# A 0/1 table multiplied onto the state decays, in place of a bias product on TensorE, in a linear-attention and Fourier-mixing kernel

## The chip, the core and the metric

The kernel runs on one core of a Trainium2 chip. The metric is device microseconds of one execution, the lower the better. A profile is one execution recorded by the hardware. Engines are named as in it: PE is TensorE (PEld its weight loads), ACT is ScalarE, DVE is VectorE, POOL is GpSimd, SP issues most DMAs.

## What is computed

Four batches, eight heads, 768 positions, 48 channels in a head (384 in all), float32 in and out. A linear attention with a decay for every channel of the key runs over the positions; its output then goes through a Fourier mixing and a two-layer network:

```python
for t in range(S):
    cur = np.einsum('bhd,bhe->bhde', u[None] * kt, vt)
    y[:, :, t] = np.einsum('bhd,bhde->bhe', rt, state + cur)
    state = wt[:, :, :, None] * state + np.einsum('bhd,bhe->bhde', kt, vt)

X = np.fft.fft(x, axis=1)
X = np.fft.fft(X, axis=2)
u = x + np.real(X)
un = (u - mean(u)) / np.sqrt(var(u) + 1e-06)
out = u + np.maximum(un @ w_ch1, 0.0) @ w_ch2
```

## The kernel before

**Chunks.** A batch is cut into six chunks of 128 positions. In a chunk the decays are summed as logarithms: a product with a triangular mask on PE gives the running sum at each position, and its exponentials scale r and k, so that the recurrence becomes three products: scores (k by r, L1120), masked by DVE (L1130); scores by v (L1185); and the state carried in from the chunk ahead, by r (L1182). The chunk's keys by its values (L1157) are added to the state in a PSUM bank, and DVE multiplies the whole with the chunk's total decay (L1165). The last chunk of a batch hands on no state.

**Total decays.** Two heads share a block of 128 partitions: the lower 64 belong to one, the upper 64 to the other. Function `total` in `attention` makes a row of eight numbers for each partition, one for each head: four products (L1006) sum the logarithms over the 128 positions, two columns at a time, and a partition gets a sum also in the column of the head it does not belong to. Ahead of them one product of the unit matrix `IDB` with a table `PB` of 0 and -200 (L1003, eight columns) writes -200 into those places, so that the exponential makes them zero. The row stands in columns 384 to 391 of the bank that holds a running sum, and ACT takes its exponential into the tail of tile `E2` (`we`), alone (L1024) or with the 384 in front of it (L1019). There are three ways for a chunk's sums, `sum_two`, `sum_add` and `sum_key`; the first uses one more product of 384 columns (L1015), the second an addition on DVE (L1029).

**Batch 0** goes in pairs of chunks (function `paired`, lines 857 to 965), with loads of two chunks each (L648) and its own bias product (L870), which is not touched. The tables of sines and the masks are made at the same time, on DVE, POOL and ACT. PE's first products (L1464, and NW products L1507 on constants) compute nothing that is used.

**After a batch's attention** follow: folding into even and odd parts (L600, `sd` and `xf`), products with cosine and sine tables (L1261, L1266), eviction and reversal (`hcs`, `hcr`, L1289 to L1293), the second transform (L1305, L1314), the sum with x, the moments (L1362, L1364), normalizing, transposing, and the two layers (L1412, then relu on ACT at L1420 or DVE at L1418, then L1431), whose result is scaled and added (L1440) and stored (L1451).

**The order.** All operations are recorded first; each engine then runs a list of them written out in the table `ORDER`, and the semaphores follow from the data. The batches overlap: while PE works at the layers of one batch, DVE, ACT and POOL do the attention of the next. For many operations the lists also choose the engine (helpers `vec`, `evict`: DVE or POOL, ACT or DVE) and the way (`choose`). An operation on POOL waits for the last DVE operation ahead of it in the plan that is marked with `port`; those are the ones that take their operands from SBUF alone. Helper lines therefore stand for many operations: L600 is every addition or product of two tensors made by `tt`, L604 and L605 are `tensor_scalar`, L611 is a fill, L614 and L623 are on ACT.

Of the kernel before, what the change touches and what calls it, by code (L numbers as in the profile page):

```python
# [7 lines left out]
ALU = mybir.AluOpType  # L8
# [26 lines left out]
NW = 8  # L35
# [31 lines left out]
    "act": (  # L67
# [385 lines left out]
def bass_rwkv6_finch__then__fnet_fourier_mix_kernel(  # L453
# [11 lines left out]
    DM = H * D  # L465
# [1075 lines left out]
```

## Time and profile before

| | |
|---|---|
| median of 3 runs | 179.47 us (179.09 to 179.93) |
| the profiled execution, its own time | 179.5 us |
| its span in the trace | 177.3 us |
| busy: PE, DVE, ACT, POOL | 171.9, 157.8, 132.5, 98.4 us |
| granted clock of TensorE | 1.00 |
| chain that ended last, by engine | PE 85%, DVE 6%, SP's queue 4%, DMA 3% |

Times in the profile count from the start of the span. The 2.2 us between the span and the time lie outside of what the trace shows. A product on PE has a "busy" time from its start to its modelled end, and products overlap; what one costs in a full stream is the distance from its start to the next one's start. A row of the chain of waits gives how long that piece held the chain.

### The profile page before, as it was taken

To read this page: it belongs to the slowest core of one execution; us is meant where nothing else is said; L and a number is where in the kernel's file an instruction comes from. 1 tells how busy PE (TensorE), PEld (TensorE's weight loads), DVE (VectorE), ACT (ScalarE), POOL (GpSimd) and SP (SyncE) were. 2 spreads that over 40 slices of the span, in tenths; PEclk is the share of its full clock that TensorE was granted. 3 is DMA by queue.
4 is the path that set the end of the run, shared out by engine and by line. 5 is a ranking of instruction groups with operands and counts; after the bars stand their busy time and mean duration, and the time that the engine had idled before them with its cause. 6 is when DMAs were issued, how large, how long until landed. Compare 5 with 4: busy or idle time off the path is not lost.

```text
span 177.3 us, 4554 instructions
## 1 busy us (share of the span) xinstructions
PE 171.9 (97%) x1704; PEld 114.4 (65%) x1704; DVE 157.8 (89%) x379; ACT 132.5 (75%) x323; POOL 98.4 (55%) x127
## 2 busy tenths in 40 slices
PE   6998999999999999999999999999999999999994
PEld 3366667866766667776667667666666775665663
DVE  8979999999999999999999998999888999683443
ACT  2899999999999986999996988897924573602400
POOL 4024359759989557599589428899376124000000
DMA  5999999999999999997998969989983123240033
GB/s 131 296 276 246 211 202 190 184 177 215 188 186 163 161 186 217 211 208 151 205 191 168 239 134 207 171 150 243 210 174 102 50 89 67 46 154 4 0 133 133
DMA packets 109031, 29.55 MB, mean 167 GB/s; under 512 B 104273, under 2 KB 109010, under 8 KB 109010
## 3 DMA queue, kind: packets, MB, share of 16 engines
q1 hardware_dynamic: 107394, 26.91, 71.5%
q0 software_dynamic: 1616, 2.36, 8.5%
q8 instruction: 13, 0.21, 0.5%
q14 instruction: 8, 0.07, 0.1%
HBM read 23.59 MB, written 4.72 MB: 160 GB/s over the span
## 4 chain that ended last, share of the span: by engine, by line
PE 85%; DVE 6%; SPq 4%; DMA 3%; issue 1%; DVEq 0%
PE bank L1431 27%; PE bank L1412 27%; PE bank L1305 5%; PE bank L1261 3%; PE bank L1120 3%; DMA in_k<-in_k_dram 3%; SPq L648 3%; PE bank L1185 2%; PE bank L1182 2%; PE bank L992 2%; DVE rkh L600 2%; PE bank L1157 2%; PE bank L1109 2%; PE bank L1097 1%; DVE ah L1130 1%; PE bank L1015 1%
## 5 line engine op out<-in xcount | busy, mean ns | idle before, releaser
L1412 PE MATMUL bank<-unt,w 128*128 128x384 bf16 x288 | 53.5, 326 | 0.0
L1431 PE MATMUL bank<-w,ht 128*128 128x384 bf16 (+2 forms) x300 | 53.2, 320 | 0.0
L1420 ACT ACTIVATE ht<-bank 128x384 bf16<-128x384 f32 x75 | 35.2, 505 | 16.2 <-PE bank L1412 16.0
L1431 PEld LDWEIGHTS bank<-w,ht 128*128 128x128 bf16 x300 | 27.7, 98 | 15.7 <-issue 0.2
L1412 PEld LDWEIGHTS bank<-unt,w 128*128 128x128 bf16 x288 | 26.7, 98 | 15.7 <-DVE rkh L1046 0.2
L1130 DVE TENSOR_TENSOR ah<-bank,msk 128x512 bf16<-128x512 f32 x47 | 30.3, 678 | 1.6 <-PE bank L1120 1.3
L600 POOL TENSOR_TENSOR rk<-rk,ub 128x384 f32<-128x384 f32 x15 | 15.0, 1000 | 5.1 <-DVE rk L600 2.6
L1418 DVE TENSOR_SCALAR ht<-bank 128x384 bf16<-128x384 f32 x21 | 10.8, 548 | 7.0 <-PE bank L1412 7.0
L1440 DVE SCALAR_TENSOR_TENSOR osb<-bank,rstd,uf 128x384 f32<-128x384 f32 (+2 forms) x22 | 13.0, 591 | 4.0 <-DMA out_dram<-osb 2.4
L623 ACT ACTIVATE rkt<-bank 128x512 bf16<-128x512 bf16 (+1 forms) x22 | 15.5, 711 | 1.2 <-PE bank L1109 0.8
L614 ACT ACTIVATE un<-uf,agg 128x384 bf16<-128x384 f32 x22 | 12.8, 618 | 3.9 <-DVE agg L1364 3.9
L600 POOL TENSOR_TENSOR rkh<-in_k,e 128x384 bf16<-128x384 f32 x13 | 13.0, 1007 | 4.6 <-DVE xf L600 2.4
L600 POOL TENSOR_TENSOR vtd<-in_v,dc 128x384 f32<-128x384 f32 x17 | 14.0, 828 | 0.8 <-DVE dc L1064 0.7
L614 ACT ACTIVATE vb<-in_v 128x384 bf16<-128x384 f32 x23 | 12.3, 543 | 2.8 <-DMA in_v<-in_v_dram 2.8
L600 POOL TENSOR_TENSOR rk<-in_r,in_k 128x384 f32<-128x384 f32 x11 | 11.0, 1008 | 2.9 <-DVE xf L600 2.8
L1185 PE MATMUL bank<-vb,ah 128*128 128x48 bf16 x192 | 11.1, 183 | 0.0
L1185 PEld LDWEIGHTS bank<-vb,ah 128*128 128x128 bf16 x192 | 9.7, 96 | 1.6 <-issue 0.4
L600 POOL TENSOR_TENSOR sd<-x 128x385 f32<-128x385 f32 x8 | 8.0, 1008 | 4.6 <-DVE rkh L600 1.9
L1196 DVE TENSOR_TENSOR x<-bank,vtd 128x384 f32<-128x384 f32 x18 | 9.8, 547 | 0.8 <-PE bank L1185 0.5
L614 ACT ACTIVATE lb<-in_w 128x384 bf16<-128x384 f32 x18 | 9.8, 544 | 0.7 <-PE bank L992 0.4
L1362 DVE BATCH_NORM_STATS2 bst<-uf 128x6 f32<-128x384 f32 x18 | 9.6, 547 | 0.2 <-POOL uf L600 0.2
L1064 DVE TENSOR_REDUCE dc<-rk 128x8 f32<-128x384 f32 x18 | 9.7, 541 | 0.0
(208 smaller groups left out, 392.0 us busy)
## 6 DMA issues: line engine op xcount, KB each, us to landing
in_v<-in_v_dram SPq DMA_DIRECT2D x24, 192.0 KB, 4.4
out_dram<-osb SPq DMA_DIRECT2D x23, 192.0 KB, 2.6
in_w<-in_w_dram SPq DMA_DIRECT2D x18, 192.0 KB, 3.9
in_r<-in_r_dram SPq DMA_DIRECT2D x18, 192.0 KB, 3.8
in_k<-in_k_dram SPq DMA_DIRECT2D x18, 192.0 KB, 4.1
in_r<-in_r_dram SPq DMA_DIRECT2D x3, 384.0 KB, 4.4
in_k<-in_k_dram SPq DMA_DIRECT2D x3, 384.0 KB, 4.5
in_w<-in_w_dram SPq DMA_DIRECT2D x3, 384.0 KB, 5.4
```

The costliest lines, as they stand in the source:

```text
L600: return lambda e: e.tensor_tensor(out=o, in0=a, in1=b, op=f)
L614: return lambda e: e.activation(o, a, f, **kw)
L623: {"act": lambda e: e.activation(o(), i(), ACTF.Copy), "dve": lambda e: e.tensor_copy(out=o(), in_=i())}, **kw)
L1064: op("dve", v_1(DM), lambda e: e.tensor_reduce(out=dc[:, :], in_=rku[:, :, :], axis=mybir.AxisListType.X, op=ALU.add), r=[("RK", i2)], w=[ ...
L1130: masked[n].append(op("dve", v_1(512), lambda e: e.tensor_tensor(out=ah[:, x:H:2, :], in0=ps(bk)[:, :].rearrange("p (h t) -> p h t", t=128 ...
L1185: ins = e.matmul(ps(ty)[:, D * h:D * h + D], ah[:, h, :], vb[:, h, :], start=first and not ype, stop=True, skip_group_check=True)
L1196: op("dve", v_1(DM), lambda e: e.tensor_tensor(out=xb[:, c, 0:DM], in0=ps(ty)[:, 0:DM], in1=vflat, op=ALU.add), r=[ty, ("VTD", n % 4)], w= ...
L1412: ins = e.matmul(ps(t)[:, 0:384], W1[:, m, 256 * (j // 2) + j % 2:256 * (j // 2) + 256:2], unt[:, :, m, :], start=(m == 0), stop=(m == NM ...
L1418: {"dve": lambda e, j=j, t=t, ht=ht: e.tensor_scalar(out=ht[:, j, :], in0=ps(t)[:, 0:384], scalar1=su, scalar2=0.0, op0=ALU.mult, op1=ALU. ...
L1420: "act": lambda e, j=j, t=t, ht=ht: e.activation(ht[:, j, :], ps(t)[:, 0:384], ACTF.Relu, scale=su)},
L1431: ins = e.matmul(ps(t)[:, 0:hi - lo], ht[:, j, 128 * x:128 * x + 128], W2[:, j, lo:hi], start=(j == 0), stop=(j == NJ - 1))
L1440: op("dve", v_1(hi - lo) + 64, lambda e: e.scalar_tensor_tensor(out=o[:, lo:hi], in0=ps(t)[:, 0:hi - lo], scalar=rstd[:, kb:kb + 1], in1=u ...
```

## The change

For batches 1 to 3 the product with `PB` is left out of `total`: the first of the two-column products starts its columns afresh. Two comparisons at the start make a table `HB` (two columns of 0 and 1, by the half that a partition lies in), and after the exponentials a product of `HB` with the eight numbers, in place, clears those of the other head; it is on POOL or DVE, as the list says. The state's update (L1165) now waits for this product. There are 15 such chunks: the lists put 14 of the products on POOL and one on DVE. Batch 0 keeps its bias product. NW goes from 8 to 9. The lists of all engines are made anew; they also choose other engines and ways for some operations: `sum_two` stands for 13 chunks in place of 12.

```diff
-NW = 8
+NW = 9
 ORDER = {
     "pe": (
-        "8 84 2367 2368 2369 2370 2371 2372 2373 2374 105 108 101 208 211 204 102 77 138 157 151 152 155 147 "
+        "8 86 2384 2385 2386 2387 2388 2389 2390 2391 2392 107 110 103 210 213 206 104 79 153 154 157 140 159 "
...
+    HB = ONES[:, 18:20]
...
+        op("dve", 62, ts(HB[:, 0:1], TC[:, 0:1], 63.5, None, ALU.is_lt), r=["TC"], w=["HB0"])
+        op("dve", 62, ts(HB[:, 1:2], TC[:, 0:1], 63.5, None, ALU.is_gt), r=["TC"], w=["HB"])
...
                 def tot(e):
-                    e.matmul(ps(t)[:, DM:DM + H], IDB[:, :], PB[:, :, :].rearrange("p h x -> p (h x)"), start=True,
-                             stop=False, skip_group_check=True)
                     for h in range(HP):
                         ins = e.matmul(ps(t)[:, DM + 2 * h:DM + 2 * h + 2],
-                                       L[:, 2 * h:2 * h + 2, :].rearrange("t h d -> t (h d)"), ONE[:, :], start=False,
+                                       L[:, 2 * h:2 * h + 2, :].rearrange("t h d -> t (h d)"), ONE[:, :], start=True,
                                        stop=True, skip_group_check=True)
                     return ins
                 if not last:
-                    op("pe", mm(1, 5), tot, r=["ONE", "IDB", "PB0", "PB", ("LB", i2)], w=[t])
+                    op("pe", mm(1, 4), tot, r=["ONE", ("LB", i2)], w=[t])
...
+            if not last:
+                w2 = we.rearrange("p (h x) -> p h x", x=2)
+                g.ctx = ("we", b, c)
+                op(None, {"pool": 90, "dve": 85}, tt(w2, w2, HB[:, :].unsqueeze(1).to_broadcast([128, HP, 2]), ALU.mult), port=("dve",),
+                   r=["HB0", "HB", ("E2", i2)], w=[("WE", i2)])
...
-        kflat, kst_k, we_k = None, [("KH", i4)], [("E2", i2)]
+        kflat, kst_k, we_k = None, [("KH", i4)], [("E2", i2), ("WE", i2)]
```

The other lines of the diff only name groups of operations. In the changed file a line stands 2 to 15 lines further down: L600 is L602, L611 is L613, L1165 is L1175.

POOL, from the last folding of batch 0 to the first products of batch 1, before (`xf` is the folding, `vtd` values by the bonus term, `w` a load of weights, `hcr` the reversed transform, `rkh` scaled keys or queries, `ah` masked scores, `vb` values in bf16, `rk` r by k):

```order
L600 TENSOR_TENSOR xf<-x 128x192 x2
L816 DMA w<-in_moe_w_ch_dram 128x3x768
L1293 COPY hcr<-hcs 128x384
L600 TENSOR_TENSOR rkh<-in_k,e_1 128x8x48
L600 TENSOR_TENSOR vtd<-in_v,dc 128x384
L600 TENSOR_TENSOR ah<-ah,msk 128x4x128
L1073 CAST vb<-in_v 128x384
L600 TENSOR_TENSOR rk<-rk,ub 128x384
```

and now, with the first three of the new products, `e_n<-e_n,ones`:

```order
L602 TENSOR_TENSOR xf<-x 128x192
L602 TENSOR_TENSOR e_0<-e_0,ones 128x8
L822 DMA w<-in_moe_w_ch_dram 128x3x768
L1304 COPY hcr<-hcs 128x384
L602 TENSOR_TENSOR rkh<-in_k,e_1 128x8x48
L602 TENSOR_TENSOR vtd<-in_v,dc 128x384
L602 TENSOR_TENSOR rk<-rk,ub 128x384
L1083 CAST vb<-in_v 128x384
L602 TENSOR_TENSOR e_2<-e_2,ones 128x8
L602 TENSOR_TENSOR ah<-ah,msk 128x4x128
L602 TENSOR_TENSOR e_1<-e_1,ones 128x8
```

The new products stand between operations that were there, and one is ahead of the mask `ah`; the rest of this piece is near to what it was.

DVE, in batch 0, from r by k of the second pair (`ht<-in_r,in_k`) to the bonus term of the first chunk, before (`sml` holds small sums of a pair, `st` the state, `un` a scratch tile):

```order
L600 TENSOR_TENSOR ht<-in_r,in_k 128x768
L600 TENSOR_TENSOR rkh<-in_r,in_w 128x8x48 x2
L600 TENSOR_TENSOR ht<-ht,ub 128x768
L920 SCALAR_TENSOR_TENSOR sml<-bank,un 128x16
L611 MEMSET rkh 128x8x8
L906 TENSOR_REDUCE sml<-ht 128x16
L1165 TENSOR_TENSOR st<-bank,sml 128x384
L1130 TENSOR_TENSOR ah<-bank,msk 128x4x128
L918 TENSOR_SCALAR un<-bank,un 128x16
L1130 TENSOR_TENSOR ah<-bank,msk 128x4x128
L920 SCALAR_TENSOR_TENSOR sml<-bank,un 128x16
L604 TENSOR_SCALAR ht<-osb 128x128
```

and now:

```order
L602 TENSOR_TENSOR ht<-in_r,in_k 128x768
L602 TENSOR_TENSOR rkh<-in_r,in_w 128x2x8x48
L606 TENSOR_SCALAR ht<-osb 128x128
L602 TENSOR_TENSOR ht<-ht,ub 128x768
L607 TENSOR_SCALAR nle<-osb 128x128
L926 SCALAR_TENSOR_TENSOR sml<-bank,un 128x16
L912 TENSOR_REDUCE sml<-ht 128x16
L1175 TENSOR_TENSOR st<-bank,sml 128x384
L613 MEMSET rkh 128x8x8
L1140 TENSOR_TENSOR ah<-bank,msk 128x4x128 x2
L606 TENSOR_SCALAR ones<-tc 128x1
L613 MEMSET rkh 128x8x8
```

The two halves of `rkh` have become one operation, the mask `nle`, the second comparison for `HB` and a second fill have come into the piece, and L918 has gone to ACT.

SP, the first loads, before:

```order
L648 DMA in_r<-in_r_dram 128x8x96
L639 DMA osb<-in_u_dram 1x384
L648 DMA in_k<-in_k_dram 128x8x96
L648 DMA in_w<-in_w_dram 128x8x96 x2
L654 DMA in_v<-in_v_dram 128x8x48
L648 DMA in_r<-in_r_dram 128x8x96
L648 DMA in_k<-in_k_dram 128x8x96
```

and now:

```order
L650 DMA in_k<-in_k_dram 128x8x96
L650 DMA in_r<-in_r_dram 128x8x96
L641 DMA osb<-in_u_dram 1x384
L650 DMA in_w<-in_w_dram 128x8x96 x2
L650 DMA in_k<-in_k_dram 128x8x96
L656 DMA in_v<-in_v_dram 128x8x48
L650 DMA in_r<-in_r_dram 128x8x96
```

The same eight loads come first; the last of them is now the second pair's r, and was its k.

More of the change, by code (lines that the diff above doesn't have):

```diff
@@ L683, in masks @@
         dset(128, ts(IDF[:, :], CI[:, 128:256], 0.0, None, ALU.is_equal), r=["CI"], w=["IDF", ("HT", 0, 0)])
+        g.ctx = "hb"
+        op("dve", 62, ts(HB[:, 0:1], TC[:, 0:1], 63.5, None, ALU.is_lt), r=["TC"], w=["HB0"])
+        op("dve", 62, ts(HB[:, 1:2], TC[:, 0:1], 63.5, None, ALU.is_gt), r=["TC"], w=["HB"])
+        g.ctx = "masks"
         op("dve", 70, ts(PB[:, :, 0], TC[:, 0:1].to_broadcast([128, HP]), 63.5, -200.0, ALU.is_gt, ALU.mult),
@@ L1042, in attention @@
             g.choose(("sum", b, c), sum_two, sum_add, sum_key)
+            if not last:
[3 more added lines that the diff above has]
+                   r=["HB0", "HB", ("E2", i2)], w=[("WE", i2)])
+                g.ctx = ("att", b, c)
             def rh_bank():
@@ L1287, in mix @@
             sg = (1.0, CP[:, :], -1.0)[j]
+            g.ctx = ("hcr", b, j)
             op(None, {"pool": 970 if j else 462, "act": a_sb(384), "dve": v_2(384)},
@@ L1294, in mix @@
                r=[("HCS", j)] + (["CP"] if j == 1 else []), w=[("HCR", j)])
+            g.ctx = ("mix", b)
         agg, lnv, rstd = AGG[i], LNV[i], RSTD[i]
@@ L1359, in add_parts @@
                         r=[("XFe", i, kb), ("XFo", i, kb)], w=[("UF", i, kb)])
+                g.ctx = ("u", b, kb)
                 g.choose(("u", b, kb), add_bank, add_row, add_parts)
+                g.ctx = ("mix", b)
                 bs = BST[n % 4]
@@ L1425, in mix @@
                 o = OSB[n % 3]
+                g.ctx = ("o", b, kb)
                 for lo, hi in ((0, DM),) if n < B * NC - 1 else ((0, 256), (256, DM)):
```

137 rows, old and new, of the table ORDER are left out of this document.

## Prediction

> **What bounds the kernel now.** I read the shares of the page first, then the busy time by stages, then the chain of waits. The page gives PE as the fullest engine, and DVE as full as PE until some 140 us (slices of 4.4 us, in tenths):
>
> ```profile
> PE 171.9 (97%) x1704; PEld 114.4 (65%) x1704; DVE 157.8 (89%) x379; ACT 132.5 (75%) x323; POOL 98.4 (55%) x127
> PE   6998999999999999999999999999999999999994
> DVE  8979999999999999999999998999888999683443
> ```
>
> The busy time by stages (columns: stretch, its length, then PE, PEld, DVE, ACT, POOL, granted clock, DMA share, GB/s) shows where PE is idle at all:
>
> ```profile
> 8.90:31.50 22.60, 21.43 (x270) 15.04 (x270) 21.64 (x47) 22.02 (x55) 12.15 (x21) 1.00 1.06 225
> 31.50:60.00 28.50, 28.50 (x338) 19.94 (x338) 27.87 (x70) 28.08 (x71) 24.02 (x29) 1.00 1.02 183
> 60.00:100.00 40.00, 40.00 (x445) 27.27 (x443) 39.57 (x84) 35.50 (x91) 29.89 (x32) 1.00 0.98 194
> 100.00:145.00 45.00, 45.00 (x438) 30.42 (x437) 42.01 (x93) 33.24 (x83) 27.42 (x31) 1.00 0.77 159
> 145.00:175.00 30.00, 29.80 (x197) 18.56 (x195) 18.78 (x46) 8.53 (x23) 3.05 (x6) 1.00 0.25 70
> ```
>
> From 31.5 us on PE has no idle time until its last product. A busy PE need not be at its full rate, so the chain of waits (start, length, what held it) is looked at too:
>
> ```profile
> 7.28 5.40 DMA in_k<-in_k_dram
> ...
> 13.64 1.02 DVE rkh L600 x2
> ...
> 24.24 0.48 DVE st L1165
> 24.72 0.05 issue
> 24.76 0.34 PE bank L1154
> ...
> 146.17 5.20 PE bank L1431 x32
> 151.37 6.34 PE bank L1412 x39
> ...
> 174.91 0.35 DVE osb L1440
> ```
>
> From 24.76 to 174.91 the chain stays on PE, and its long pieces run at 6.34/39 = 0.163 us a product of 384 columns. So there are two parts: up to about 25 us a load and then DVE decide, and from there the sum of PE's products. A saving counts in full if it shortens PE's list after 25 us; a saving on DVE, ACT or POOL counts for nothing there as long as PE never waits; and a new order cannot win anything after 31.5 us but by less PE work. It can lose.
>
> **The change part by part.** *The removed product.* PE's timeline at one of the 15 places:
>
> ```profile
> 37.01 0.24 PE L1264 MATMUL bank<-sn,xf 128*128 128x193 bf16 x1
> 37.09 0.17 PE L1003 MATMUL bank<-ones,idw 128*128 128x8 bf16 x1
> 37.12 0.24 PE L1006 MATMUL bank<-ones,lb 128*128 128x2 bf16 x4
> 37.22 0.24 PE L1263 MATMUL bank<-ss,xf 128*128 128x193 bf16 x1
> ```
>
> Start to start L1003 takes 37.12 - 37.09 = 0.03 us; its weights are loaded beside the product ahead of it. 15 x 0.03 = 0.45 us less. At the least it is 0 (if the next product had to wait for its own weights anyway), at the most 15 x 0.055 = 0.8 us, a whole weight change as between transposes (the chain has four of them in 0.22 us). I take 0.45, the row of the thing itself.
>
> *One more product of 384 columns.* The groups before have L1015 twelve times; the lists now make 13:
>
> ```profile
> L1015 PE MATMUL bank<-lb,nle 128*128 128x384 bf16 x12 | 3.9, 326 | 0.0
> ```
>
> That is 0.163 us more on PE (start to start, from the chain above). The numbers of transposes, and the rest of PE's list, are the same, and the runs of score products (L1120) that stand between other products are 17 in both lists.
>
> *The ninth constant product.* It comes at the start, where PE waits next:
>
> ```profile
> 7.52 1.48 PE L1507 MATMUL bank<-idw,msk 128*128 128x384 bf16 x8 [0.29 <-DVE msk L604]
> 9.16 2.11 PE L857 MATMUL bank<-uf,un 128*128 128x384 bf16 x12 [0.17 <-ACT uf L614]
> ```
>
> The eight would be followed by the ninth 0.163 us later, and it would end at about 9.16, when L857 gets its logarithms from ACT. ACT covers it: 0. Without that cover it costs 0.16.
>
> *The start on DVE.* The timeline has the gate, and the chain the sizes:
>
> ```profile
> 12.77 0.96 DVE L600 TENSOR_TENSOR ht<-in_r,in_k 128x768 f32<-128x768 f32 x1 [0.96 <-DMA in_k<-in_k_dram]
> 15.68 0.07 DVE rkh L611
> 17.62 0.14 DVE un L918
> 18.50 0.13 DVE ht L604
> 18.63 0.87 DVE rkh L600
> ```
>
> DVE waits until 12.77 us for the second pair's data and is then nearly full to 31.5 us. The gate is the last of the same first eight loads, so I leave it where it is. Between the gate and the last addition of batch 0's outputs DVE loses L918 twice (2 x 0.14) and has one operation of 0.87 in place of two halves (1.02): 0.43 less. It gains the mask `nle` and a comparison for `HB` (about 0.14 each, as L604) and one fill (0.07): 0.35 more. Nothing is left of it: between -0.1 and +0.1.
>
> *The 15 new products.* No row shows one of eight numbers. On POOL the two sizes that it has give a line:
>
> ```profile
> L600 POOL TENSOR_TENSOR rk<-rk,ub 128x384 f32<-128x384 f32 x15 | 15.0, 1000 | 5.1 <-DVE rk L600 2.6 <-DVE sd L600 2.1
> L600 POOL TENSOR_TENSOR xf<-x 128x191 bf16<-128x191 f32 x4 | 2.4, 592 | 0.0
> L611 POOL MEMSET x<- 128x24 f32 x2 | 0.2, 118 | 0.0
> ```
>
> (1000 - 592)/193 = 2.1 ns a number, so 592 - 183 x 2.1 = 0.2 us for eight (an estimate; a fill of 24 numbers takes 0.12). 14 x 0.2 = 2.8 us on POOL, which has 4.5 us free between 31.5 and 60 us and 10 between 60 and 100. DVE's one is about 0.14, as L918. The bounds for the path are 0, if each is done while DVE is at something else, and the whole 2.8, if DVE stands still for each. Behind the new product on POOL stand that chunk's keys, its bonus term or a mask (the pieces of the order above); for it waits L1165 on DVE, the state's update. In the lists the DVE operation that lets each of the 14 go stands 15 or more operations ahead of the L1165 that reads it. I take 0.
>
> *What else the lists move.* Of two-input operations of 384 numbers DVE has nine fewer (0.55 each, the row below) and one more of 768 (0.87): -4.1 us; three more from a bank, one last addition more and smaller ones give back about 1.3. So DVE has some 2.8 us less to do, POOL some 5 more beside the 2.8. On the path this is 0, since PE does not wait there; it is room for DVE where it has 0.6 us in 28.5 and 0.4 in 40.
>
> ```profile
> L600 DVE TENSOR_TENSOR xf<-sd 128x382 bf16<-128x382 f32 (+1 forms) x13 | 6.6, 548 | 0.0
> ```
>
> *The sum.* -0.45 + 0.16 + 0 + 0 + 0 = -0.3 us, with +0.1 for one or two short waits that a new order puts in: -0.2. Against the execution with 179.5 us, which is as good as the median (179.47), that is 179.3 us.
>
> **The rivals.** *A. POOL's new products hold DVE up (slower).* Two operations that take all from SBUF, one on POOL and one on DVE, do not run beside each other here. The group of DVE's `rkh`, and the timeline with POOL at a product until 59.47 and DVE starting one at 59.22:
>
> ```profile
> L600 DVE TENSOR_TENSOR rkh<-in_k,e 128x384 bf16<-128x384 f32 x5 | 2.9, 571 | 0.0
> ...
> 57.51 1.96 POOL L600 TENSOR_TENSOR rk<-in_r,in_k 128x384 f32<-128x384 f32 x2
> 59.22 0.67 DVE L600 TENSOR_TENSOR rkh<-in_k,e 128x384 bf16<-128x384 f32 x1
> ```
>
> DVE's took 0.67 instead of 0.55 (the mean of the five, 0.571, is that of four at 0.55 and this one). If each new product stops DVE for its 0.2 us and POOL's further 5 us stop it for a part, say a fifth, DVE loses 2.8 + 1.0 = 3.8 us, 1.0 more than it has gained; it runs out of its 0.6 us between 31.5 and 60 us, where the first five of the new products lie, and what is late there (keys, masks, state) makes PE wait. I put that at 0.4 to 2.5 us: middle 1.5, 180.8 us. It decides from the point at which DVE's lost time in that stage passes its idle 0.6 and its share of the relief. Against it: POOL's operations wait for the DVE operation marked ahead of them, so that of the five only this one was stretched. The Trainium skill (SBUF — State Buffer, section SBUF: two separate sides) says that DVE and GpSimd share a port pair as an exclusive lock, held for a whole instruction, and that a DVE operation with two SBUF inputs is blocked in full by a GpSimd operation that reads. The stretched 0.67 us agrees with that rule; a sum that charges every new product to DVE by it would be A's.
>
> *B. The start gets shorter (faster).* The first pair's k and r are now the first two loads, with the small one behind them, and the second pair's k is ahead of a v. If that brings the gate at 12.77 forward, DVE's wait of 0.96 us goes, and all behind it moves: at most -0.9 more, 178.4 us. For it: DVE is the chain from there on. Against it: the gate needs r as well as k, and r is still the eighth of the same loads.
>
> *C. The removed product was free, and only the additions count.* Then +0.16 for L1015 and 0.16 for the ninth constant product are left, 179.8 us. Against it are the 0.03 us between the starts of L1003 and L1006.
>
> **How the numbers follow.** A measurement of this kernel tells 0.5%, 0.9 us, from no change: faster is below 178.6, slower above 180.4. The sum's own case has 0.47, with a range of its own of 178.9 to 179.9, and C has 0.18: both lie within. A has 0.22, since an order made anew has nothing to win after 31.5 us and something to lose; B has 0.13. Of A a quarter stays below 180.4 and of B a quarter above 178.6, which makes 0.10 faster, 0.73 same, 0.17 slower. The range is to hold 8 in 10: it goes down to B's 178.4 and up to 181.0, a little beyond A's middle; half of B and some four tenths of A are left out, 0.15 together.
>
> **What would show it.** Right: the group of the eight-column product has only batch 0's kind left; L1015 stands 13 times; PE is again without idle time from about 31.5 us; the last product ends 0.1 to 0.4 us earlier; the new products take 0.1 to 0.3 us on POOL, and no DVE operation's longest wait names them. Wrong: idle time of PE or gaps between L1412 or L1431 after 31.5 us; DVE waiting for POOL at L1175; two-input operations of DVE that take 0.6 us or more in larger numbers (A); the second pair's product on DVE starting more than 0.3 us away from 12.77 (B, or its opposite).

## The result and the profile after

The changed kernel takes 177.84 us (median of 11 executions, 177.74 to 179.02), the kernel before 179.18 (11 executions beside it, 178.88 to 179.93): a ratio of 0.9932, 95% interval 0.9912 to 0.9953. That is 1.3 us faster, below the range that was forecast. The profiled execution took 177.74 us with a span of 175.9, against 179.5 and 177.3. Medians and ratios, here and in the table of the experiments, leave out executions more than 1.5% above the lowest of the same kernel (none in this comparison; below, nine of the kernel before, one each of four experiments, that of old_loads with 977.78 us, and five of the last one).

The page of the changed kernel, its shares and slices (4.4 us each, in tenths):

```profile
PE 171.5 (97%) x1691; PEld 114.4 (65%) x1691; DVE 156.0 (89%) x374; ACT 130.9 (74%) x320; POOL 104.9 (60%) x145
PE   6999999999999999999999999999999999999994
DVE  7999999999999999999999999999899599826253
```

They look like the old ones: PE lost 0.4 us of busy time and is as full as it was. What moved is in the stages (the columns as in the prediction) and in the start.

```profile
8.90:31.50 22.60, 22.00 (x284) 15.23 (x283) 22.32 (x51) 22.48 (x58) 13.07 (x20) 1.00 1.07 224
31.50:60.00 28.50, 28.50 (x338) 20.27 (x337) 28.17 (x67) 28.50 (x75) 24.18 (x34) 1.00 1.01 182
60.00:100.00 40.00, 40.00 (x431) 27.20 (x430) 39.31 (x85) 34.62 (x85) 33.15 (x41) 1.00 0.94 194
145.00:175.00 30.00, 28.41 (x187) 17.63 (x185) 16.51 (x38) 8.09 (x21) 2.26 (x4) 1.00 0.30 86
```

From 8.9 to 31.5 us PE did 284 products in place of 270, though the lists took products away, and DVE is busy for 22.32 us in place of 21.64. The timeline of DVE has the second pair's r by k at 11.63 us, with no wait in brackets behind it (12.77 with 0.96 before), and the chain of waits begins with ACT where it began with a load:

```profile
11.63 0.95 DVE L602 TENSOR_TENSOR ht<-in_r,in_k 128x768 f32<-128x768 f32 x1
```

```profile
8.38 1.47 ACT uf L616 x2
...
29.33 0.94 ACT lb L616 x2
...
172.42 1.01 PE bank L1446 x15
173.43 0.03 issue
173.46 0.02 DVEq L403
173.48 0.04 issue
173.52 0.35 DVE osb L1455
```

The gate of the start is gone. Until some 31 us ACT decides, then PE to the end, which comes 1.39 us earlier (173.52 against 174.91). The groups of the added operations:

```profile
L1019 PE MATMUL bank<-lb,nle 128*128 128x384 bf16 x13 | 4.2, 326 | 0.1
L602 POOL TENSOR_TENSOR e<-e,ones 128x8 f32<-128x8 f32 x14 | 2.8, 206 | 2.7 <-DVE e L602 2.7
```

L1019 (the old L1015) stands 13 times, and a new product takes POOL 0.206 us.

**Where the 1.4 us of span came from.** A landmark helps: the first product of the second transform (L1305, now L1317). Ahead of it PE's two lists hold the same products, but for four L1003 and one L1015 more before, and the ninth constant product now.

```profile
37.98 1.31 PE L1305 MATMUL bank<-dtm,hcs 128*128 128x384 bf16 x7
```

```profile
36.95 0.82 PE L1317 MATMUL bank<-dtm,hcs 128*128 128x384 bf16 x4
```

It comes 1.03 us earlier. The other 0.37 us lie behind it. From the start of a chunk's totals to the next product PE takes 0.133 us before and 0.105 now (means of the 15 places, from the starts in both traces), so the removed product is worth 0.028 each. That gives, in us:

| | ahead of the landmark | behind it | sum |
|---|---|---|---|
| removed products, 4 and 11 | -0.11 | -0.31 | -0.42 |
| L1015, one fewer and two more | -0.16 | +0.33 | +0.16 |
| what is left | -0.76 | -0.39 | -1.15 |
| all | -1.03 | -0.37 | -1.40 |

The first two rows count every product in full, which is an upper bound for those ahead of some 30 us, where ACT decides. Each column is from one execution of each kernel, and that of the kernel before is 0.3 us above its median, so a part of the last row may be spread. With that said, the sum's two products were right, and some 1.15 us are not in it. The experiments are about these.

### The profile page after: what moved, and what is told of

Read it like the earlier page. It is cut to its first block, busy times and chain, and to the rows that moved or that the text cites. A ratio compares the mean times of both kernels' runs of the same rounds, so it can differ in the third digit from the quotient of the medians.

```text
span 175.9 us, 4537 instructions
## 1 busy us (share of the span) xinstructions
PE 171.5 (97%) x1691; PEld 114.4 (65%) x1691; DVE 156.0 (89%) x374; ACT 130.9 (74%) x320; POOL 104.9 (60%) x145
## 4 chain that ended last, share of the span: by engine, by line
PE 81%; ACT 14%; DVE 2%; issue 1%; ACTq 0%; DVEq 0%
PE bank L1446 27%; PE bank L1426 27%; PE bank L1317 5%; PE bank L1271 4%; ACT rkt L625 3%; PE bank L1130 3%; PE bank L1195 2%; PE bank L1119 2%; PE bank L998 2%; PE bank L1192 2%; PE bank L1167 1%; ACT vb L616 1%; ACT uf L892 1%; ACT in_w L888 1%; ACT uf L616 1%; PE bank L1019 1%
## 5 line engine op out<-in xcount | busy, mean ns | idle before, releaser
L625 ACT ACTIVATE rkt<-bank 128x512 bf16<-128x512 bf16 (+1 forms) x22 | 16.4, 796 | 0.9 <-PE bank L1107 0.7
L602 POOL TENSOR_TENSOR xf<-sd 128x382 bf16<-128x382 f32 (+1 forms) x11 | 10.8, 1002 | 10.2 <-DVE sd L602 7.5
L602 POOL TENSOR_TENSOR rkh<-in_k,e 128x384 bf16<-128x384 f32 x15 | 15.0, 1006 | 2.4 <-DVE rk L602 1.5
L602 POOL TENSOR_TENSOR rk<-in_r,in_k 128x384 f32<-128x384 f32 x14 | 13.9, 1002 | 0.8 <-DVE vtd L602 0.8
L602 POOL TENSOR_TENSOR vtd<-in_v,dc 128x384 f32<-128x384 f32 x17 | 14.2, 835 | 0.4 <-DVE dc L1074 0.3
L602 POOL TENSOR_TENSOR rk<-rk,ub 128x384 f32<-128x384 f32 x13 | 13.0, 1005 | 2.0 <-DVE rk L602 2.0
L616 ACT ACTIVATE vb<-in_v 128x384 bf16<-128x384 f32 x23 | 12.9, 569 | 1.2 <-DMA in_v<-in_v_dram 1.2
L1206 DVE TENSOR_TENSOR x<-bank,vtd 128x384 f32<-128x384 f32 x19 | 10.4, 547 | 0.8 <-PE bank L1195 0.7
L1192 PE MATMUL bank<-st,rkt 128*128 128x96 bf16 x80 | 9.7, 204 | 0.0
```

What stands on the lines that cost most here:

```text
L602: return lambda e: e.tensor_tensor(out=o, in0=a, in1=b, op=f)
L616: return lambda e: e.activation(o, a, f, **kw)
L625: {"act": lambda e: e.activation(o(), i(), ACTF.Copy), "dve": lambda e: e.tensor_copy(out=o(), in_=i())}, **kw)
L1192: e.matmul(ps(ty)[:, 96 * q:96 * q + 96], rT[:, q, :], s_in[:, q, :], start=not ype, stop=False, skip_group_check=True)
L1206: op("dve", v_1(DM), lambda e: e.tensor_tensor(out=xb[:, c, 0:DM], in0=ps(ty)[:, 0:DM], in1=vflat, op=ALU.add), r=[ty, ("VTD", n % 4)], w= ...
```

## The experiments

The theory: the order of the first loads moved the gate. Its rivals: the new order of the engines did it, or the product itself is worth more than its 0.03 us. Later calls add how the table's products stand to DVE. The five calls ran on four chips, where the kernel before is slower than above and spreads more, so times are compared inside a call, and the places in the traces across all. The columns: median and lowest time; in how many of all its executions the granted clock of TensorE, a mean over the execution, is 0.99 and not 1.00; the median of before in the same call, and the ratio to it with its interval; what SP takes to issue the two loads of w; the start of the second pair's r by k on DVE; the landmark.

| kernel | median, lowest | at 0.99 | before | ratio | w | DVE | landmark |
|---|---|---|---|---|---|---|---|
| before | 179.18, 178.88 | | | | 2.48 | 12.77 | 37.98 |
| changed | 177.84, 177.74 | 1 of 11 | 179.18 | 0.9932 (0.9912 to 0.9953) | 1.38 | 11.63 | 36.95 |
| old_loads | 179.21, 178.39 | 4 of 12 | 180.25 | 0.9950 (0.9920 to 0.9979) | 2.75 | 12.26 | 37.61 |
| new_loads | 178.91, 178.45 | 0 of 6 | 180.25 | 0.9930 (0.9903 to 0.9957) | 1.40 | 11.51 | 37.10 |
| bias_back | 178.36, 178.07 | 0 of 6 | 180.25 | 0.9890 (0.9866 to 0.9914) | 1.21 | 11.63 | 37.02 |
| undone | 178.46, 178.25 | 0 of 5 | 180.25 | 0.9895 (0.9873 to 0.9917) | 1.43 | 11.38 | 36.72 |
| after_again | 178.23, 177.78 | 1 of 6 | 180.42 | 0.9865 (0.9816 to 0.9914) | 1.80 | 11.63 | 36.96 |
| only_order | 180.78, 179.40 | 5 of 12 | 180.42 | 0.9999 (0.9964 to 1.0035) | 2.59 | 12.42 | 37.77 |
| hb_thrice | 179.57, 178.96 | 0 of 12 | 180.42 | 0.9939 (0.9910 to 0.9969) | 1.76 | 11.63 | 36.96 |
| v_late | 178.39, 178.01 | 0 of 6 | 180.42 | 0.9874 (0.9827 to 0.9921) | 1.74 | 11.63 | 37.23 |
| old_three | 179.46, 178.25 | 7 of 12 | 179.88 | 0.9967 (0.9936 to 0.9998) | 2.78 | 12.11 | 37.45 |
| old_five | 177.92, 177.76 | 1 of 11 | 179.88 | 0.9922 (0.9894 to 0.9950) | 1.72 | 11.63 | 36.97 |
| no_we | 178.55, 178.30 | 0 of 12 | 179.88 | 0.9937 (0.9911 to 0.9963) | 1.83 | 11.63 | 36.97 |
| nw8 | 177.81, 177.76 | 1 of 12 | 179.88 | 0.9912 (0.9884 to 0.9939) | 1.38 | 11.63 | 36.97 |
| r_k_u | 178.54, 177.77 | 0 of 12 | 180.28 | 0.9907 (0.9869 to 0.9945) | 1.89 | 11.63 | 36.95 |
| k_u_r | 180.16, 178.55 | 7 of 12 | 180.28 | 0.9999 (0.9958 to 1.0040) | 3.24 | 12.65 | 37.98 |
| only_wait | 178.45, 177.80 | 1 of 10 | 180.28 | 0.9910 (0.9874 to 0.9945) | 1.80 | 11.63 | 36.99 |
| order_and_table | 179.65, 178.94 | 5 of 12 | 180.28 | 0.9968 (0.9935 to 1.0001) | 2.47 | 13.56 | 38.95 |
| w_next | 177.76, 177.73 | 0 of 5 | 179.60 | 0.9895 (0.9866 to 0.9926) | 1.60 | 11.62 | 36.94 |
| w_early | 179.06, 178.06 | 5 of 12 | 179.60 | 0.9945 (0.9911 to 0.9978) | 1.60 | 11.63 | 36.96 |

**The loads, all eight.** SP's two loads of w, in the kernel before and in the changed one:

```profile
2.22 2.48 SPq L648 DMA_DIRECT2D in_w<-in_w_dram  x2
```

```profile
2.67 1.38 SPq L650 DMA_DIRECT2D in_w<-in_w_dram  x2
```

The edit of old_loads; new_loads has (2, 0, 1, 3, 4, 7, 5, 6) in the kernel before:

```diff
-    g.schedule(ORDER)
+    g.schedule(ORDER); s = g.order["sp"]; s[:8] = [s[i] for i in (1, 2, 0, 3, 4, 6, 7, 5)]
```

> The changed kernel with its first eight loads in the order of before (r, u, k, w, w, v, r, k in place of k, r, u, w, w, k, v, r); every other list, wait and bank is as in the changed kernel. Theory L (the order of the loads moved the gate of the start): the second pair's r by k on DVE goes from 11.63 us back to 12.4 to 12.9 us, DVE waits there again for 0.6 to 1.0 us, and the time is 0.5 to 0.9 us above the changed kernel's 177.84: 178.3 to 178.7 us. Rival O (the new order of DVE and ACT made the start shorter, the loads only go along): under 0.2 us, 177.8 to 178.0. Rival P (the whole gain is the product taken off PE): 177.8.

> The kernel before with its first eight loads in the order of the changed kernel (k, r, u, w, w, k, v, r); nothing else is different. Theory L: the second pair's r by k on DVE starts at 11.6 to 12.0 us instead of 12.77, and the time falls by 0.5 to 0.9 us, to 178.3 to 178.7 from 179.18; if ACT, which has only 0.6 us of idle time between 8.9 and 31.5 us, becomes the bound of the start, the gain stops at some 0.6. Rival O: DVE starts earlier but something else in the old order of the start is late next, and the time stays within 0.2 of 179.18. Rival P: 179.18.

In the changed kernel the old loads bring the gate back to 12.26 us and the landmark to 37.61: 0.66 of the 0.76 us. In the kernel before, the new loads bring the landmark forward by 0.88 us, but the span falls by 0.4 only (177.3 to 176.9). The waits of new_loads show a good part of why:

```profile
PEld bank L1431 <- DMA w<-in_moe_w_ch_dram: 0.8, 2, 0.5
```

The second layer's weights now come after PE, which they did not before; PE has two more waits at 74 and 75 us. Rivals O and P fall: with nothing but the first eight loads exchanged the start moves in both kernels.

**Which of the loads.** All are permutations of the same kind: old_three (1, 2, 0), r_k_u (1, 0, 2), k_u_r (0, 2, 1), old_five (0, 1, 2, 3, 4, 6, 7, 5), v_late (0, 1, 2, 3, 4, 5, 7, 6).

> The changed kernel with only its first three loads in the order of before (r, u, k in place of k, r, u); the second pair's k stays ahead of v. Which part of the new order of loads brings the gate forward? Theory T (the small load between the two large ones): the two loads of w take SP 2.4 to 2.8 us again instead of 1.4 to 1.8, the gate goes back to 12.2 us or later, and the time rises by most of what all eight cost, 0.5 to 1.2 us above the changed kernel. Rival F (the place of v ahead of both of the second pair's loads): the issue of w stays short and the time within 0.3 us.

> The changed kernel with the last three of its first eight loads in the order of before (v, r, k in place of k, v, r), the first three left as they are. Theory T: w's issue stays at 1.4 to 1.8 us, the gate at 11.4 to 11.8, the time within 0.2 us of the changed kernel. Rival F: the gate goes to 12.2 or later, 0.5 us or more above it.

> The changed kernel with its first three loads as r, k, u: the large ones first as now, but r ahead of k as before. Theory U (the small load between the two large ones holds up what SP issues behind it): the two loads of w take SP 1.4 to 1.9 us, DVE is at the second pair's product at 11.63 us without a wait, and the time is the changed kernel's, 177.8 to 178.0. Rival R (k has to be ahead of r): w takes 2.5 to 2.8 us, the product starts at 12.1 or later, and the time is that of the kernel with r, u, k, some 179.4.

> The changed kernel with its first three loads as k, u, r: k first as now, the small load between as before. Theory U: w takes 2.5 to 2.8 us, the second pair's product starts at 12.1 us or later, some 179.4 us. Rival R: as the changed kernel, 177.8 to 178.0.

> The changed kernel with the v of chunk 0 issued behind the second pair's r instead of ahead of it (k, r, u, w, w, k, r, v); nothing else is different. In the changed kernel DVE no longer waits at the second pair's product: it comes to it at 11.63 us and the data is there. Theory (the gate is gone; from 8.4 us on ACT and DVE are the bound): the same time within 0.2 us, or slower by up to 0.3 if ACT's cast of v is late. Rival (the loads still set the start): faster by 0.3 to 0.6 us, as the data comes some 0.6 us earlier.

SP's timeline of k_u_r, and below it that of r_k_u:

```profile
0.74 0.46 SPq L650 DMA_DIRECT2D in_k<-in_k_dram  x1
1.26 0.46 SPq L641 DMA_DIRECT2D osb<-in_u_dram  x1
1.78 0.40 SPq L650 DMA_DIRECT2D in_r<-in_r_dram  x1
2.22 3.24 SPq L650 DMA_DIRECT2D in_w<-in_w_dram  x2
5.51 1.15 SPq L650 DMA_DIRECT2D in_k<-in_k_dram  x1
```

```profile
1.26 0.56 SPq L650 DMA_DIRECT2D in_k<-in_k_dram  x1
1.87 0.47 SPq L641 DMA_DIRECT2D osb<-in_u_dram  x1
2.39 1.89 SPq L650 DMA_DIRECT2D in_w<-in_w_dram  x2
4.32 1.15 SPq L650 DMA_DIRECT2D in_k<-in_k_dram  x1
```

It is the place of u. With 1.5 KB between the two loads of 384 KB, the issue of w takes 2.5 to 3.2 us and everything behind it leaves some 0.6 to 1.2 us later; with u third it takes 1.2 to 1.9. Where DVE feels it differs. The kernel before waits 0.32 us at the first pair's product (6.16 us) and 0.96 at the second's; in old_loads and only_order, too, a part falls on each. old_three, k_u_r and order_and_table have no wait at the second; they wait at the first, for the large load that left behind u, and all that follows moves. The first pair's product in old_three, and in the changed kernel:

```profile
6.23 0.96 DVE L602 TENSOR_TENSOR uf<-in_r,in_k 128x768 f32<-128x768 f32 x1 [0.62 <-DMA in_k<-in_k_dram]
```

```profile
5.52 0.95 DVE L602 TENSOR_TENSOR uf<-in_r,in_k 128x768 f32<-128x768 f32 x1
```

So the change moved two waits and not one. Which of k and r is first, and whether v stands ahead of the second pair's k, changes nothing (r_k_u 36.95, old_five 36.97). The rate at which data come in shows the same, in steps of 0.4 us, before and after:

```profile
GB/s 0 0 0 0 27 132 240 325 283 221 197 293 300 324 317 305 313 323 298 266 235 280 299 319 248 266 294 272 314 324 303 272 176 118 154 291 322 259 164 189
```

```profile
GB/s 0 0 0 0 38 138 185 324 326 323 326 325 323 328 323 325 327 324 322 326 321 265 270 307 325 318 275 289 308 275 269 120 215 203 108 165 276 304 302 324
```

Before, it sinks to 197 at 4 us while SP is held at w, and again to 235 at 8 us; after, it stays at 321 or more from 2.8 to 8.4 us. Why u does that, and whether the slow issue lowers the rate or the low rate holds the issue, no trace shows. v_late confirms that the gate no longer binds: DVE starts at 11.63 whatever comes earlier, and the landmark is 0.28 later.

In time it is 1.6 us between k_u_r and r_k_u, and old_three is 1.5 above old_five, more than the landmarks' 1.03 and 0.48. The column "at 0.99" shows what was added: with u second the new order runs at that clock in 28 of 60 executions, and with u third, w_early apart, it is 5 of 114; the kernel before has 26 of 123 in the five calls. old_three's five executions at 1.00 take 178.25 to 178.76 us, its seven at 0.99 179.42 to 180.19. The only trace of an execution at 0.99 is that of order_and_table. Its constant products, and the stretch around them in the stages' columns; below them the same products in old_three, which has the same order of loads:

```profile
8.40 2.95 PE L1522 MATMUL bank<-idw,msk 128*128 128x384 bf16 x9 [2.03 <-DVE idw L606]
7.70:11.10 3.40, 2.70 (x9) 1.31 (x10) 3.40 (x18) 2.07 (x4) 0.89 (x2) 0.50 1.09 259
```

```profile
8.10 1.64 PE L1522 MATMUL bank<-idw,msk 128*128 128x384 bf16 x9 [0.83 <-DVE idw L606]
```

PE waits for a table that DVE makes behind the first pair's product, 2.03 us there, and the granted clock is 0.50 from 7.7 to 11.1 us; the landmark comes 1.50 us after old_three's. That the wait lowers the clock is likely but not shown, since it is one trace. It also means that the row of order_and_table (13.56 and 38.95) is not the loads alone.

**The product and the order.** bias_back puts the bias product back and keeps the table (the first edit). undone has that and takes the table and its products out (the second). only_order is undone with the loads of old_loads, and order_and_table is bias_back with those of old_three.

```diff
+                    e.matmul(ps(t)[:, DM:DM + H], IDB[:, :], PB[:, :, :].rearrange("p h x -> p (h x)"), start=True, stop=False, skip_group_check=True)
                     for h in range(HP):
-                        ins = e.matmul(ps(t)[:, DM + 2 * h:DM + 2 * h + 2],
-                                       L[:, 2 * h:2 * h + 2, :].rearrange("t h d -> t (h d)"), ONE[:, :], start=True,
+                        ins = e.matmul(ps(t)[:, DM + 2 * h:DM + 2 * h + 2], L[:, 2 * h:2 * h + 2, :].rearrange("t h d -> t (h d)"), ONE[:, :], start=False,
...
-                    op("pe", mm(1, 4), tot, r=["ONE", ("LB", i2)], w=[t])
+                    op("pe", mm(1, 4), tot, r=["ONE", "IDB", "PB0", "PB", ("LB", i2)], w=[t])
```

```diff
     g.schedule(ORDER)
+    for h in [o for o in g.ops if o.key[0] == "hb" or o.key[0][0] == "we"]:
+        g.order[h.eng].remove(h)
+        g.ops.remove(h)
+        for o in g.ops:
+            if h in o.deps:
+                o.deps = o.deps - {h} | h.deps
     g.emit()
```

> The changed kernel with the product of the unit matrix and the table of 0 and -200 put back ahead of the four sums, 15 times; the products with the 0/1 table stay, so the decays are cleared twice. Theory: 15 products at 0.023 to 0.03 us of PE, nothing else moves: 0.35 to 0.45 us above 177.84, 178.2 to 178.3. Rival P (the whole gain is this product): 179.0 to 179.2. Rival C of the prediction (the product was free): 177.8.

> The changed kernel with the bias product back and with the 15 products with the 0/1 table and the two comparisons that make it left out: the old arithmetic in the new order, same result. Theory: the products with the table cost nothing on the path, since POOL does them while DVE is at other things, so 178.2 to 178.3 as with the bias product alone put back. Rival A of the prediction (each new product stops DVE for its 0.2 us and some of that reaches PE): 0.3 us or more below the kernel that has both, 177.9 or less. And if the gain came from the changed arithmetic and not from the order, this kernel falls back to 179.0 or more.

> The changed kernel with the bias product back, the products with the 0/1 table and its comparisons left out, and the first eight loads in the order of before: of the change only the new order of the engines is left; same result. Theory (three parts that add: loads 0.7, product 0.35, and 0.3 to 0.4 of short waits of PE that the old order had after 31.5 us and the new one has not): 0.3 to 0.4 us below the kernel before and about 1.0 above the changed kernel, 178.8 to 179.0. Rival (order counts for nothing, the two kernels differ by loads and product alone): the same as the kernel before.

> The changed kernel with the bias product back beside the products with the table, and its first three loads in the order of before: what differs from the kernel before is the rest of the new order and the table's products. Theory (the rest of the new order is worth 0.3 to 0.4 us of short waits of PE after 31.5 us): 0.3 us or more below the kernel before in the same call, and its last product some 0.3 us earlier in the trace than there (174.3). Rival (the rest of the new order is worth nothing; the gain is loads and product): within 0.2 us of the kernel before, last product at 174.2 to 174.6.

The lowest time of bias_back is 0.33 us above the changed kernel's, near the 0.42 that 15 products of 0.028 make. undone, with the old arithmetic throughout, is about as fast as bias_back (its lowest time is 0.18 above) and still 1.8 us below the kernel before of its call: most of the gain is not the changed arithmetic. That it is level with bias_back hides two things that its trace shows. Without the first of the two comparisons for `HB`, which stands at 2.04 us in the changed kernel, a small operation of DVE starts 0.06 us earlier and takes half the time, and all that follows in the start is 0.25 us earlier (DVE 11.38). And PE waits for `xf` at 71 us, 0.54 us from one start to the next where the stream has 0.05; the runs of the next part show why. The small operation, in the changed kernel and in undone, and PE's wait in undone:

```profile
2.17 0.36 DVE L606 TENSOR_SCALAR ones<-tc 128x2 bf16<-128x2 f32 x1
```

```profile
2.11 0.17 DVE L606 TENSOR_SCALAR ones<-tc 128x2 bf16<-128x2 f32 x1
71.36 0.33 PE L1271 MATMUL bank<-cs,xf 128*128 128x193 bf16 x2 [0.33 <-DVE xf L602]
```

only_order has the new order of all engines, but the old first loads and the old arithmetic, and stands level with the kernel before: my 0.3 to 0.4 us for the rest of the order did not come in its time. It cannot decide, though: it has lost the table's products as well, PE waits for `xf` at 72 us just as in undone, and five of its twelve executions are at 0.99. order_and_table, which keeps the products, has 0.9968, with an interval that reaches 1.0001, and again five at 0.99. Most of the 0.39 us behind the landmark are four gaps of 0.06 to 0.09 us in PE's old stream, which the changed kernel's does not have; what the rest of the order is worth in time stays open.

**The table's products and DVE.** hb_thrice makes two more products of each into a scratch row, no_we takes them out (the loop above with "we" alone), only_wait puts a fill of four numbers of a scratch tile `SCR` in their place:

```diff
-                op(None, {"pool": 90, "dve": 85}, tt(w2, w2, HB[:, :].unsqueeze(1).to_broadcast([128, HP, 2]), ALU.mult), port=("dve",),
+                op(None, {"pool": 90, "dve": 85}, fill(SCR[:, n % 6, :], 0.0), port=("dve",),
```

> The changed kernel with each of the 15 products with the 0/1 table done three times, twice into a scratch row and then in place: 28 more operations of 0.2 us on POOL, two more on DVE. Theory (POOL does them while DVE is at other things and has 13 us free up to 145 us): 0 to 0.2 us above the changed kernel. Rival A (each stops DVE for its time): DVE loses up to 5.6 us more, has 0.3 us free between 31.5 and 60 us, and the time rises by 0.5 to 3 us.

> The changed kernel with the 15 products with the 0/1 table left out and no bias product in their place: the decays of the other head are not cleared, so the state's update uses them as they are; all else is as in the changed kernel. Doing each product three times cost 1.3 us. If that cost is linear in the operations (each holds up the keys behind it on POOL or DVE), leaving them out gains 0.5 to 0.7 us: 177.2 to 177.4. If there is a point from which it costs (idle time of POOL and DVE takes the first 15), the time is that of the changed kernel within 0.2 us, as putting them in beside the bias product also changed nothing (178.36 with, 178.46 without).

> The changed kernel with each of the 15 products with the 0/1 table replaced by a fill of four numbers in a scratch row, in the same places of the lists and with the same waits; the decays of the other head are not cleared. Theory G (it is the wait in POOL's queue for the DVE operation marked ahead of it that keeps POOL's next product off DVE's two-input ones): as the changed kernel, 177.7 to 178.0, no DVE operation stretched at 70 us, and no wait of PE at 71. Rival (the products' time or data matter): the 178.5 of the kernel without them.

Of hb_thrice the stage in which the first five of them lie:

```profile
31.50:60.00 28.50, 28.48 (x336) 20.18 (x335) 27.93 (x66) 28.50 (x75) 25.72 (x43) 1.00 1.01 181
```

28 more products on POOL (and two on DVE) cost 1.5 us of span (177.4 against 175.9), all behind the landmark, most of it in five waits of PE of 0.19 to 0.31 us. POOL is busy for 25.72 us there in place of 24.18, and what stands behind on it (keys, values, a load of weights that leaves at 57.48 in place of 56.57) is later. To leave the products out costs as well, 0.5 us at the lowest times (178.30 against 177.76 and 177.76 of its neighbours), against both of my cases. The timelines of DVE and POOL at 70 us, of no_we:

```profile
70.18 1.24 DVE L602 TENSOR_TENSOR xf<-sd 128x384 bf16<-128x384 f32 x1
```

```profile
69.63 1.37 POOL L602 TENSOR_TENSOR rkh<-in_k,e 128x384 bf16<-128x384 f32 x1 [0.93 <-DMA in_k<-in_k_dram]
```

and of the changed kernel:

```profile
70.16 1.03 DVE L602 TENSOR_TENSOR xf<-sd 128x384 bf16<-128x384 f32 x2
71.40 0.20 POOL L602 TENSOR_TENSOR e<-e,ones 128x8 f32<-128x8 f32 x1 [2.73 <-DVE e L602]
71.56 1.00 POOL L602 TENSOR_TENSOR rkh<-in_k,e 128x384 bf16<-128x384 f32 x1
```

In the changed kernel POOL waits 2.73 us for DVE's own product with the table, and the keys behind it start when DVE's two `xf` are done (1.03 us for both). Without it the keys start at 69.63, inside DVE's work: one `xf` takes 1.24 us instead of 0.55, the keys 1.37 instead of 1.00, and PE has to wait for `xf`:

```profile
71.56 0.33 PE L1271 MATMUL bank<-cs,xf 128*128 128x193 bf16 x2 [0.37 <-DVE xf L602]
```

The Trainium skill (SBUF — State Buffer, section SBUF: two separate sides) says that of a DVE operation with two inputs in SBUF and a GpSimd operation that reads there, the one that starts first gets the shared ports for the whole instruction and the other is blocked in full. The trace agrees: the keys end at 71.00, and `xf`, which started at 70.18, ends 0.42 us after them. In only_wait the two `xf` take 1.03 us again and its lowest time is 177.80: the wait in POOL's queue, not the multiplication, keeps the two apart. Its median, 178.45, is that of no_we and not that of the changed kernel; its trace has other waits (of PE's loads of operands 1.4 us for relu, 0.6 for weights). So that the wait does it is shown by the traces and the lowest time, and not by the median.

**The ninth constant product.**

> The changed kernel with eight constant products at the start instead of nine. Theory: the ninth lies in PE's wait for the logarithms from ACT, so the time is the same within 0.1 us. Rival: it costs its 0.16 us, and the time falls by that; or it keeps PE busy ahead of its first real work, and the time rises.

Nothing, as the prediction had it.

**What is late next.** The changed kernel's executions reach 179.4 us. w_next and w_early move POOL's last loads of weights ahead in its list; the edit of w_next:

```diff
-    g.schedule(ORDER)
+    g.schedule(ORDER); q = g.order["pool"]; q.insert(55, q.pop(57))
```

> The changed kernel once more, unchanged, as the measure for the others, since on the last chip the kernel before had a median of 180.27 us instead of 179.2 and a spread from 179.1 to 182.6. If the spread comes from the old order of loads (whose kernels alone showed it), this one stays between 177.7 and 178.3; if it comes from the chip, it spreads as well and lies near 178.8.

> The changed kernel with POOL's last load of weights issued right behind the one ahead of it, two operations earlier (at 54.8 us instead of 56.57); nothing else is different. Theory W (the late third of the weights makes PE wait at 63 to 64 us in some executions): it lands some 1.8 us earlier, no wait of PE for it in the trace, the fast executions stay at 177.75 and those above 178.5 go or become rarer: median 177.7 to 177.9. Rival (the two loads of weights share the bandwidth, so that the pair lands no earlier, or the loads of SP behind them land later): no change in the spread, or 0.2 us slower.

> The changed kernel with POOL's last two loads of weights issued three and four operations earlier (some 3 us); nothing else is different. Theory W: as with the one load, with 3 us to spare: median 177.7 to 177.9, no execution above 178.3 for this cause. Rival: the loads of r and k for the next chunks, which SP issues in the same stretch, land later, and DVE or POOL wait for them: 0.2 to 0.5 us slower.

The chain of after_again, whose span is 0.4 us longer with the same landmark, and the wait in it:

```profile
55.64 0.94 POOL rk L602
56.58 6.79 DMA w<-in_moe_w_ch_dram
63.37 0.05 issue
63.42 0.66 PE bank L1446 x3
```

```profile
PEld bank L1446 <- DMA w<-in_moe_w_ch_dram: 0.5, 1, 0.5
```

With the load issued next to the one ahead of it, this wait is gone from the trace, and five executions lie between 177.73 and 177.97. It beats the kernel before by 1.05% and is level with the changed kernel at its best; whether its upper executions are gone is not shown, since of 40 executions of the four kernels that start alike (changed, after_again, old_five, nw8) 29 lie below 178.5 as well, and five of five are little against that; of the eleven above, four are at 0.99. w_early goes too far, with a median 1.3 us above w_next's: the loads of k and v then come late.

```profile
DVE rk L602 <- DMA in_k<-in_k_dram: 1.0, 1, 1.0
ACT vb L616 <- DMA in_v<-in_v_dram: 1.0, 1, 1.0
```

## Why the prediction was wrong

- **The removed product**: -0.45 forecast, -0.42 by the starts in the traces, -0.33 by the lowest times of bias_back. Right; so rival C is out.
- **One more L1015**: it is there, 13 times; its 0.16 was not measured apart. **The ninth constant product**: 0, as nw8 shows.
- **The start**: this step failed. "The gate is the last of the same first eight loads, so I leave it where it is" took the landing of a load from its place in the list. The place was the same, but what SP needed for the loads ahead of it was not: 2.48 us for the two of w became 1.38, and the gate went from 12.77 to before 11.63. DVE's wait of 0.32 us at the first pair's product, which went too, had no term at all. The trace of before showed it: that row of SP's, and the dip of the data rate beside it, were part of the chain (the load of k and SP's queue, 7% of it), and I read only how long DVE waited. Measured: 0.66 us by old_loads, 0.76 by the ledger, where rival B had at most 0.9.
- **Rival B** was what happened, at a chance of 0.13, and for one of the two reasons that it gave: old_five shows that the second pair's k ahead of v does nothing; u behind k and r does it.
- **The 15 new products at nothing, and rival A**: 0.206 us each against 0.2, and no cost on the path. What the table did cost is the first of its two comparisons, 0.25 us at the start by undone's trace; the sum has only the other, behind the gate, at 0.14. A's mechanism is real, as no_we's 1.24 us show, but the products work against it: their wait keeps POOL's keys off DVE. I had that wait as an argument against A; that it also pays I had not.
- **Waits that a new order puts in**: +0.1 forecast, -0.39 in the two traces. "A new order cannot win anything after 31.5 us but by less PE work" was too strong: a PE without idle time still had gaps of 0.06 to 0.09 us that the slices don't show. That the order as such closed them is argued from the traces; no time shows it.

## What to carry to other kernels

Read the issue of the first loads as part of the critical chain: a small load between large ones cost this kernel 0.5 to 1 us at the start, and some executions 1.3 us more through the clock, and moving it one place back was worth more than the arithmetic that the change is named for. Before an operation off the path is removed, look at whom its wait keeps apart: here 0.2 us of work on POOL also kept two engines out of each other's way. And where a start moves forward, look for what was just in time: in new_loads half of the gain was lost again, a good part of it to the weights of a layer some 50 us later.

## What the runs showed of the hardware

- With a load of 1.5 KB as the second of SP's queue, the issue of the two large loads behind the next one takes 2.5 to 3.2 us instead of 1.2 to 1.9 (six kernels against fourteen), and the rate of data dips: to 197 GB/s in the kernel before, to 278 in only_order, while the changed kernel stays at 321 or more. No run shows why.
- Two operations on SBUF, one on POOL, one on DVE, block each other: in no_we 1.24 us for one of 0.55 on DVE, and 1.37 for one of 1.00 on POOL.
- From issue to landing a load of 384 KB by POOL's queue takes 4.6 to 7.7 us beside SP's loads (twenty traces). PE's loads of operands wait nothing for it in the changed kernel, 0.5 us in after_again and 1.1 us in r_k_u.
- In the one trace of an execution with a mean clock of 0.99, the granted clock is 0.50 for 3.4 us after PE had stood idle for 2.03 us. The seven executions of old_three at 0.99 are 1.3 us above its five at 1.00, by their medians.
